# Linear attention with elu features: the first head's k loaded through ScalarE's DMA queue, at the same moment as its q through SyncE's

## Chip, cores, metric

One core of one Trainium2 chip. The metric is device time in microseconds (us), lower is better; a run counts as slow here when it is more than 1.5% above the fastest of its kernel. Positions such as "at 12 us" are counted from the start of the profiled span.

## The reference, cut

```
q, k, v: bf16 [1, 32 heads, 2048, 128]
phi_q = where(q > 0, q + 1, exp(q)) + 1e-6
phi_k = where(k > 0, k + 1, exp(k)) + 1e-6
kv  = einsum("bhsd,bhse->bhde", phi_k, v);   z = sum over s of phi_k
out = (phi_q @ kv) / (phi_q . z + 1e-6)
```

The kernel writes phi as min(exp(x), 1) + 1e-6 plus relu(x), so each head needs, for k and for q, an exponential (ACT), a min (DVE) and a relu.

## The kernel before: what matters here

Each engine has a fixed list of operations; waits are worked out from dependencies.

The operations (h is the head), with the line of the profile of before; in the profiles of the changed kernel each line number is higher by one:

```
ld*  SP    512 KB load into one of 7 buffers                         L324
T    PE    16 transposes of q                                        L368
eq   ACT   exp of the transposed q (PSUM)                            L372
ek   ACT   exp of k                                                  L336
em   DVE   min of k's exp (SBUF to SBUF)                             L339
emq  DVE   min of q's exp (SBUF to SBUF)                             L374
rkd  DVE   relu of k, first half (SBUF to SBUF)                      L342
rkp  POOL  relu of k, second half                                    L346
v1   POOL  copy of v beside a column of ones; for h >= 3 it also waits for r(h-3).0    L350
kv   PE    phi_k^T [v 1];   kvs ACT copies it to SBUF                L357, L362
n    PE    phi_q [kv z]; needs kvs and "ones"                        L389, L394, L396
r, f DVE   reciprocal; multiply (PSUM to SBUF)                       L403, L410
```

## Time and profile before

| | before |
|---|---|
| time, median of the runs of the first measurement | 170.62 us (169.57 to 170.72, 6 runs) |
| profiled run | 169.65 us, span 168.3 us |
| PE idle from 26 to 160 us | none |
| q, k, v of head 0 land | 4.2, 5.4, 7.7 us |

PE, DVE and ACT are all over 90% busy. From 26 us on PE never waits, so the end moves with whatever happens before that. The prediction below shows the lines.

### The profile page before, as it was taken

Reading aid. Unit: us, or ns where it says so; the run is one execution under the profiler, and the core shown is the slowest. Engines: PE = TensorE matmul, PEld = TensorE weight load, DVE = VectorE, ACT = ScalarE, POOL = GpSimd, SP = SyncE. Lnnn points to the kernel's source line nnn. Section 1 sums busy time; section 2 is a strip of 40 time slices with the busy share of each in tenths; the row PEclk is TensorE's granted clock in tenths of the full one; section 3 lists DMA queues with packets and bytes.
Section 4 is the critical chain, followed back from the end, with each engine's and each line's share of the span. In section 5 each row is a group of like instructions: output and inputs, shape, how many; then the busy total and the mean of one; then the engine's idle time right before and its main releaser. Section 6 shows DMA issues by size and latency. Waiting matters only on the chain.

```text
span 168.3 us, 6310 instructions
## 1 busy us (share of the span) xinstructions
PE 159.4 (95%) x2775; PEld 154.1 (92%) x2775; DVE 153.8 (91%) x267; ACT 153.7 (91%) x133; POOL 87.1 (52%) x71
## 2 busy tenths in 40 slices
PE   6999789999999999999999999999999999999960
PEld 2679779999999999999999999999999999999950
DVE  0177999999999999999999999999999999999894
ACT  3699989999999999999999999999999999998710
POOL 1436925556655555556555566556655565445000
PEclk9999999999999999999999999999999999999997
DMA  5999999999999999999999999999999999999986
GB/s 195 383 416 420 404 407 409 410 407 409 416 409 412 416 413 417 417 414 422 407 418 413 414 420 413 412 419 414 419 416 420 413 415 420 412 416 417 395 332 253
DMA packets 18748, 67.53 MB, mean 401 GB/s; under 512 B 2080, under 2 KB 2464, under 8 KB 18720
## 3 DMA queue, kind: packets, MB, share of 16 engines
q1 hardware_dynamic: 18720, 67.12, 98.9%
q8 instruction: 22, 0.36, 0.8%
q14 instruction: 6, 0.05, 0.1%
HBM read 50.33 MB, written 16.78 MB: 399 GB/s over the span
## 4 chain that ended last, share of the span: by engine, by line
PE 85%; DVE 8%; ACT 4%; issue 1%; POOL 0%; POOLq 0%
PE la L357 32%; PE la L394 18%; PE la L396 16%; PE la L368 16%; DVE la L410 4%; ACT la L336 2%; PE la L315 2%; DVE la L342 1%; DVE la L339 1%; ACT la L372 1%; PE la L389 1%; DVE la L403 1%; DVE la L381 1%; ACT la L378 1%; POOL la L301 0%
## 5 line engine op out<-in xcount | busy, mean ns | idle before, releaser
L410 DVE TENSOR_TENSOR la<-la 128x1536 bf16<-128x1536 f32 (+2 forms) x65 | 77.6, 1195 | 0.2
L396 PE MATMUL la<-la 128*128 128x129 bf16 x512 | 68.1, 220 | 0.0
L394 PE MATMUL la<-la 128*128 128x129 bf16 x512 | 68.0, 219 | 0.0
L372 ACT ACTIVATE la<-la 128x2048 bf16<-128x2048 bf16 (+2 forms) x35 | 60.3, 1732 | 5.7 <-PE la L368 3.8
L357 PE MATMUL la<-la 128*128 128x129 bf16 x1024 | 64.0, 219 | 0.7 <-DVE la L339 0.7
L350 POOL COPY la<-la 128x1024 int32<-128x1024 int32 (+1 forms) x33 | 41.9, 1273 | 38.1 <-DVE la L403 28.8
L336 ACT ACTIVATE la<-la 128x2048 bf16<-128x2048 bf16 (+1 forms) x33 | 61.4, 1863 | 0.0
L357 PEld LDWEIGHTS la<-la 128*128 128x128 bf16 x1024 | 60.0, 97 | 1.2 <-DVE la L339 0.8
L346 POOL TENSOR_SCALAR la<-la 128x1024 bf16<-128x1024 bf16 x32 | 44.5, 1393 | 29.1 <-DVE la L410 25.0
L396 PEld LDWEIGHTS la<-la 128*128 128x128 bf16 x512 | 49.5, 97 | 0.0
L394 PEld LDWEIGHTS la<-la 128*128 128x128 bf16 x512 | 47.1, 97 | 0.0
L368 PE MATMUL la<-la 128*128 128x128 bf16 x512 | 34.3, 221 | 0.4 <-DVE la L381 0.4
L389 PE MATMUL la<-la 128*128 128x3 bf16 (+1 forms) x192 | 32.3, 168 | 2.3 <-DVE la L410 1.6
L378 ACT ACTIVATE la<-la 128x1024 bf16<-128x1024 bf16 (+1 forms) x32 | 33.6, 1049 | 0.0
L368 PEld LDWEIGHTS la<-la 128*128 128x128 bf16 x512 | 29.9, 99 | 1.3 <-DVE la L381 0.5
L339 DVE TENSOR_SCALAR la<-la 128x2048 bf16<-128x2048 bf16 (+1 forms) x33 | 23.0, 696 | 3.6 <-ACT la L336 3.6
L389 PEld LDWEIGHTS la<-la 128*128 128x128 bf16 x192 | 18.7, 97 | 3.1 <-DVE la L410 2.0
L342 DVE TENSOR_SCALAR la<-la 128x1024 bf16<-128x1024 bf16 x32 | 17.1, 535 | 4.6 <-DMA la<-in_k_dram 4.6
L374 DVE TENSOR_SCALAR la<-la 128x2048 bf16<-128x2048 bf16 (+2 forms) x35 | 20.9, 599 | 0.3 <-ACT la L372 0.3
L381 DVE TENSOR_SCALAR la<-la 128x1024 bf16<-128x1024 bf16 x31 | 20.8, 671 | 0.0
L403 DVE RECIPROCAL la<-la 128x12 f32<-128x12 f32 (+2 forms) x65 | 12.8, 197 | 2.5 <-PE la L396 1.3
L362 ACT ACTIVATE la<-la 128x129 bf16<-128x129 f32 x32 | 9.1, 283 | 0.4 <-PE la L357 0.4
(14 smaller groups left out, 11.7 us busy)
## 6 DMA issues: line engine op xcount, KB each, us to landing
la<-in_q_dram SPq DMA_DIRECT2D x32, 512.0 KB, 15.5
la<-in_k_dram SPq DMA_DIRECT2D x32, 512.0 KB, 15.3
la<-in_v_dram SPq DMA_DIRECT2D x32, 512.0 KB, 15.3
out_dram<-la SPq DMA_DIRECT2D x31, 512.0 KB, 15.2
out_dram<-la SPq DMA_DIRECT2D x2, 192.0 KB, 2.5
out_dram<-la SPq DMA_DIRECT2D x1, 128.0 KB, 2.4
```

What stands on the lines that cost most here:

```text
L336: add("ACT", f"ek{h}.{i}", lambda e, a=a, b=b: e.activation(em_sb[:, h % NE, a:b], k_sb[:, h % NI, a:b], ACT.Exp), over("ldk", h, ld_parts ...
L339: add("DVE", f"em{h}.{i}", lambda e, a=a, b=b: e.tensor_scalar(em_sb[:, h % NE, a:b], em_sb[:, h % NE, a:b], 1.0, EPS, op0=ALU.min, op1=AL ...
L346: add("POOL", f"rkp{h}.{i}", lambda e, a=a, b=b: e.tensor_scalar(rk_sb[:, h % NR, a:b], k_sb[:, h % NI, a:b], BIG, 0.0, op0=ALU.min, op1=A ...
L350: add("POOL", f"v1{h}.{i}", lambda e, a=a, b=b: e.tensor_copy(v1_sb[:, h % NV, a:b, 0:D].bitcast(i32), v_sb[:, h % NI, a:b].bitcast(i32)), ...
L357: ins = e.matmul(kv_ps, lhsT=src[:, j], rhs=v1_sb[:, h % NV, j, 0:NC], start=(j + part == 0), stop=(j == NT - 1 and part == 1))
L368: ins = e.transpose(xT[:, j], q_sb[:, h % NI, j], ident[:])
L372: add("ACT", f"eq{h}.{i}", lambda e, a=a, b=b: e.activation(emq_sb[:, h % NQ, a:b], xT[:, a:b], ACT.Exp), over("T", h, t_parts, a, b) + fr ...
L378: add("ACT", f"rqa{h}", lambda e: e.activation(rq_sb[:, h % NQ, 0:n], xT[:, 0:n], ACT.Relu), over("T", h, t_parts, 0, n) + freed(NQ, h, (" ...
L389: e.matmul(_ap(o_ps[:, :], o + D, [[NC, m]]), lhsT=ones[:], rhs=epsr[:, 0:m], start=True, stop=False, skip_group_check=True)
L394: e.matmul(to, lhsT=emq_sb[:, h % NQ, t], rhs=kvs_sb[:, h % NK], start=False, stop=False, skip_group_check=True)
L396: ins = e.matmul(to, lhsT=rq_sb[:, h % NQ, t], rhs=kvs_sb[:, h % NK], start=False, stop=True, skip_group_check=True)
L410: return e.tensor_tensor(out=_ap(o_sb[:, :, :, :], first(o_sb[:, h % NO, t0, 0:1]) - first(o_sb[:, :, :, :]), [[m * D, nb], [D, m], [1, D] ...
```

## The change

The intent: q and k of head 0 are the first two things that are needed, and SyncE issues them one after the other, 0.42 us apart. ScalarE is free at the start, so it issues k at the moment at which SyncE issues q.

```diff
+BY_ACT = ('ldk0.0',)
 "ACT":
-        eq0.0 eq0.1 ek0.0 ek0.1 rqa0 ...
+        ldk0.0 eq0.0 eq0.1 ek0.0 ek0.1 rqa0 ...
 "SP":
-        ldq0.0 ldk0.0 ldv0.0 ldk1.0 ...
+        ldq0.0 ldv0.0 ldk1.0 ...
 def load(name, dst, src, h, i, t0, t1, last):
-            add("SP", f"ld{name}{h}.{i}", ...
+            add("ACT" if f"ld{name}{h}.{i}" in BY_ACT else "SP", f"ld{name}{h}.{i}", ...
```

More of the change, by code (lines that the diff above doesn't have):

```diff
@@ L115 @@
     "ACT": """
-        eq0.0 eq0.1 ek0.0 ek0.1 rqa0 ek1.0 kvs0 eq1.0 rqa1 ek2.0 kvs1 ek3.0 eq2.0 rqa2 kvs2 ek4.0 eq3.0 kvs3 rqa3
+        ldk0.0 eq0.0 eq0.1 ek0.0 ek0.1 rqa0 ek1.0 kvs0 eq1.0 rqa1 ek2.0 kvs1 ek3.0 eq2.0 rqa2 kvs2 ek4.0 eq3.0 kvs3 rqa3
         ek5.0 eq4.0 kvs4 rqa4 ek6.0 eq5.0 kvs5 rqa5 ek7.0 eq6.0 kvs6 rqa6 ek8.0 eq7.0 kvs7 rqa7 ek9.0 eq8.0 kvs8
@@ L132 @@
     "SP": """
-        ldq0.0 ldk0.0 ldv0.0 ldk1.0 ldq1.0 ldv1.0 ldk2.0 ldq2.0 ldk3.0 ldv2.0 ldv3.0 ldk4.0 ldq3.0 ldv4.0 ldq4.0
+        ldq0.0 ldv0.0 ldk1.0 ldq1.0 ldv1.0 ldk2.0 ldq2.0 ldk3.0 ldv2.0 ldv3.0 ldk4.0 ldq3.0 ldv4.0 ldq4.0
         ldk5.0 ldv5.0 ldk6.0 ldq5.0 ldv6.0 ldv7.0 ldk7.0 ldq6.0 ldk8.0 ldq7.0 ldk9.0 ldk10.0 ldq8.0 ldv8.0 ldv9.0
@@ L323, in load @@
         def load(name, dst, src, h, i, t0, t1, last):
-            add("SP", f"ld{name}{h}.{i}", lambda e: e.dma_start(dst[:, h % NI, t0:t1], rows(src, h)[:, t0:t1]),
+            add("ACT" if f"ld{name}{h}.{i}" in BY_ACT else "SP", f"ld{name}{h}.{i}", lambda e: e.dma_start(dst[:, h % NI, t0:t1], rows(src, h)[:, t0:t1]),
                 last, dma=f"{name}{h % NI}.{i}")
```

## The prediction

> **What bounds the kernel now.** I read the page first, then the table of stretches (busy time of each engine in each piece of the span), then the timeline of the first 24 us, then the landings of single DMAs.
>
> The page names PE as the chain that ended last, but three engines are almost equally full:
>
> ```profile
> PE 159.4 (95%) x2775; PEld 154.1 (92%) x2775; DVE 153.8 (91%) x267; ACT 153.7 (91%) x133; POOL 87.1 (52%) x71
> PE 85%; DVE 8%; ACT 4%; issue 1%; POOL 0%; POOLq 0%
> q1 hardware_dynamic: 18720, 67.12, 98.9%
> ```
>
> The table of stretches says where the slack is (columns: stretch, us, then busy us of PE, PEld, DVE, ACT, POOL, clock, DMA share, GB/s):
>
> ```profile
> 6.00:10.00 4.00, 4.00 (x33) 2.26 (x32) 0.84 (x3) 4.00 (x5) 1.94 (x3) 1.00 1.02 405
> 10.00:14.00 4.00, 3.59 (x66) 3.44 (x64) 2.75 (x10) 4.00 (x4) 2.41 (x2) 1.00 1.03 420
> ...
> 18.00:22.00 4.00, 3.34 (x58) 3.02 (x55) 4.00 (x5) 3.64 (x3) 2.87 (x3) 1.00 1.02 409
> 22.00:26.00 4.00, 3.47 (x60) 3.27 (x60) 3.96 (x8) 3.73 (x3) 1.16 (x2) 1.00 1.04 411
> ...
> 30.00:60.00 30.00, 30.00 (x551) 29.95 (x549) 29.80 (x52) 30.00 (x27) 17.68 (x13) 1.00 1.03 411
> ```
>
> From 26 us to 160 us PE has no idle time, so what moves the end is the moment at which PE becomes full, about 23.7 us. The change touches the first microseconds only. There ACT is the bound: from its first exponential at 5.80 us on it works without a pause until 21.6 us. What started it is in the timeline (start us, duration, engine, line, and in brackets the idle time before and who ended it):
>
> ```profile
> 0.74 0.37 SPq L324 DMA_DIRECT2D la<-in_q_dram  x1
> 1.16 0.42 SPq L324 DMA_DIRECT2D la<-in_k_dram  x1
> 1.53 3.38 PE L315 MATMUL la<-la 128*128 128x480 bf16 x8 [1.53 <-POOL la L301]
> 4.30 0.15 PEld L368 LDWEIGHTS la<-la 128*128 128x128 bf16 x1 [0.25 <-DMA la<-in_q_dram]
> 4.70 1.67 PE L368 MATMUL la<-la 128*128 128x128 bf16 x16
> 5.80 1.94 ACT L372 ACTIVATE la<-la 128x1024 bf16<-128x1024 bf16 x2 [3.78 <-PE la L368]
> 7.62 2.00 ACT L336 ACTIVATE la<-la 128x1024 bf16<-128x1024 bf16 x2
> ...
> 5.45 0.43 DVE L342 TENSOR_SCALAR la<-la 128x1024 bf16<-128x1024 bf16 x1 [4.55 <-DMA la<-in_k_dram]
> ```
>
> (The last line stands earlier in the timeline, by its start.) The reader is to see a chain: q of head 0 lands, PE transposes it (L368), ACT takes its exponential (L372), and only then, in ACT's fixed order, the exponential of k (L336) at 7.62. The landing times by tile are 3.5 us after issue for q (0.74 + 3.5 = 4.2 us), 4.3 for k (1.16 + 4.3 = 5.4) and 6.1 for v (1.63 + 6.1 = 7.7). So q has next to no slack: the weight load that needs it starts at 4.30, on the 0.40 us beat of the warm-up matmuls before it. k is used by ACT only at 7.62, and has 7.62 - 5.45 = 2.2 us of slack there; only two early relu halves (DVE L342 and GpSimd L346) start on its landing, and neither is on the chain.
>
> [...] The trace of before uses one data queue only (q1, 18720 packets)[...] it does show the engines full, 369 GB/s in 2.5 to 3 us and 401 GB/s in 3 to 4 us, so two transfers at once can't both be as fast as one alone. [...] the relu half of L342 takes 0.43 us at 5.45 and 1.26 us at 17.27 beside a GpSimd copy. [...] the 128x480 warm-up matmuls start 0.40 us apart at first, and 15 of them take 3.20 us (0.21 each) after 6.21.
>
> **The change, part by part.** It moves one instruction of 512 KB: k of head 0 leaves SyncE's list (second place) and becomes ACT's first instruction. Nothing is added; the count of DMAs and bytes stays. The instruction order of PE, DVE and GpSimd is the same.
>
> (1) Issue: k's issue moves from 1.16 to about 0.74 us, 0.42 us earlier, and every later SyncE issue comes about 0.45 us earlier. The DMA engines have work in hand from 1.8 us on (0.67 busy by 2.5 us, 1.01 in 3 to 4), so earlier issue brings at most a quicker ramp: in 1.8 to 3.0 us, at the 401 GB/s seen later, about 480 KB could move; seen are 0.4 us at 92, 0.5 at 221 and 0.5 at 369, or 332 KB. The lack of 150 KB is 0.37 us; I expect 0.1 to 0.2 of it back.
>
> (2) ACT: its table load (1.28 us, at 0.73 before) starts some 0.4 us later and ends near 2.5 us. Its first use is at 5.80: no cost.
>
> (3) q: now the two transfers start together and share. One DMA alone takes 512 KB / 0.41 MB per us = 1.28 us of the 16 engines. [...] q ends where the pair ends, at k's old landing of 5.42 less the ramp gain: 5.2 to 5.4 us, against 4.2 before. k gains nothing: it lands there too. v, third, has the same bytes ahead of it: 7.6 to 7.7 as before.
>
> (4) PE: the first transpose needs q. It starts at 4.91 in the chain of waits (4.70 in the timeline, under the last warm-up matmul). With q at 5.3 it starts at about 5.4, some 0.5 to 0.7 us late. Eight transposes at half clock take 0.87 us as before; ACT's first exponential starts at 6.3 to 6.5 in place of 5.80. So ACT's whole first stretch is **0.6 us late** (0.5 to 0.8).
>
> (5) What of it reaches the end. ACT works without idle to 21.6 us, so kvs, the first output matmuls and DVE's first reciprocal (14.32) shift by 0.6. But between 16.7 and 21.1 us DVE and GpSimd alternate: the GpSimd copy at 16.71 is released by the landing of the third head's v, which this change doesn't move, and DVE's L342 (1.26 where 0.43 is the free length), L339 (1.52, free 0.68) and L342 again (1.25) lose 0.83 + 0.84 + 0.82 = 2.5 us to it and its two successors. With DVE 0.6 us later, more of that copy lies beside DVE's PSUM work, which it doesn't disturb, so up to 0.6 us may be swallowed. ACT then has idle time of 0.44 (before L362 at 22.07) and 0.20 (before L372 at 24.35) that can take up 0.64 us if DVE isn't late. I take half as swallowed: of 0.6 us some 0.3 to 0.4 reaches PE's full stretch, and from there the end, unshortened. DMA doesn't gain or lose: it is full anyhow and buffered seven heads deep.
>
> Sum: 170.63 + 0.4 = **171.0 us**, or +0.2%.
>
> **Rivals.** (a) *SyncE's descriptors arrive first on all 16 engines*[...]. Then q lands at 4.2 to 4.3 as before, k at 5.4 or a little earlier, and nothing changes: 170.4 to 170.8. For it: ACT may take longer to issue than SyncE. Against: both are released from the starting barrier at the same moment (ACT's table load 0.73, SyncE's issue 0.74). (b) *All of the delay reaches the end*, or ACT's share goes first: +0.7 to +1.0, 171.3 to 171.6. For it: ACT and PE have no slack before 21 us in the table of stretches. Against: the GpSimd alternation above. (c) [...] a gap of half a microsecond in PE's warm-up, at 4.9 to 5.4 us[...]. Then the 15 warm-up matmuls ahead of the first kv take up to 0.40 in place of 0.21 us each, and the first kv (9.35 us) slips by up to 2 us: about 172.3. [...] (d) *Faster*: k early helps the chain. I see nothing for it: k is not awaited on the chain, and even a whole microsecond gained at the head would be 0.6%.
>
> **Range and chances.** Weights: partly swallowed 0.45 (around 171.0), no delay 0.2 (170.6), all of it 0.25 (171.4)[...]. The runs of before spread from 170.01 to 170.72, so a median of few runs is uncertain by 0.3. That gives 170.2 to 171.9 for 8 in 10. A change of 2% would be 3.4 us, which no rival reaches: faster 0.01, same 0.98, slower 0.01.
>
> **What would show the steps right or wrong.** Step 3 is right if q lands about 4.5 us after its issue (3.5 before), and k at 5.2 to 5.4 us; wrong if q still lands near 4.2. Step 4: ACT's first L372 starts at 6.3 to 6.5. Step 2: the table load ends by 3 us. Step 5: compare the start of kvs of the third head (L362 at 22.07) and of the last DVE multiply with ACT's lateness: if they are late by the full 0.6, nothing was swallowed; if by none, all was. The warm-up matmuls after the transposes must still take about 0.21 us each, else (c). The prediction is wrong if q is not delayed and the time still changes by over 0.5 us, or if the steady stretch from 26 us on shows PE idle.

## More of the kernel before

The starts of the lists (cuts marked with ...):

```
"PE":   w2 w1 T0.0 T0.1 w0 kv0.0 kv0.1 T1.0 n0.0 kv1.0 ...       # w: warm-up matmuls, WARM = (15, 4, 4)
"DVE":  v1ones0 rkd0.0 em0.0 eps0 em0.1 v1ones1 emq0.0 rqb0.0 emq0.1 eps1 rkd1.0 eps2 ones em1.0 r0.0 ...
        ... r24.1 rqb26.0 f24.1 r25.0 rkd28.0 emq26.0 f25.0 ...
"ACT":  eq0.0 eq0.1 ek0.0 ek0.1 rqa0 ek1.0 kvs0 eq1.0 ...
"POOL": ident0 ident rkp0.0 v10.0 v10.1 v11.0 rkp1.0 rkp2.0 v12.0 ...
"SP":   ldq0.0 ldk0.0 ldv0.0 ldk1.0 ldq1.0 ldv1.0 ...
```

One more view is needed afterwards: the timeline of DVE and GpSimd around 12 us in the kernel before (start us, duration us, engine, line, operation; in brackets the idle time before it and who ended it).

```profile
11.29 0.42 DVE L342 TENSOR_SCALAR la<-la 128x1024 bf16<-128x1024 bf16 x1
...
12.60 2.48 POOL L346 TENSOR_SCALAR la<-la 128x1024 bf16<-128x1024 bf16 x2
...
14.32 0.23 DVE L403 RECIPROCAL la<-la 128x12 f32<-128x12 f32 x1 [1.14 <-PE la L396]
```

DVE's relu of head 1 is over at 11.7 us, before GpSimd's relus begin at 12.60. The first reciprocal, which marks the end of the first group of head 0's output matmuls, starts at 14.32.

## The result

171.62 us median (171.50 to 171.86, 6 runs) against 170.62: ratio 1.0075, 95% interval 1.0048 to 1.0101. Ratios here are the mean time of one kernel's fast runs over that of the other's in the same rounds, so not quite the ratio of the quoted medians. The change makes the kernel slower by about 1 us, inside the range and within 2%, but by more than the 0.4 us predicted.

The page of the changed kernel, its busy shares and its queues (queue 10 is new, the k of head 0):

```profile
PE 159.0 (93%) x2775; PEld 153.4 (90%) x2775; DVE 155.1 (91%) x267; ACT 153.8 (90%) x133; POOL 86.5 (51%) x71
...
q10 hardware_dynamic: 144, 0.52, 0.8%
```

The start, in the timeline of the changed kernel:

```profile
0.73 0.40 ACTq L325 DMA_DIRECT2D la<-in_k_dram  x1
...
0.74 0.37 SPq L325 DMA_DIRECT2D la<-in_q_dram  x1
...
5.47 1.13 PE L369 MATMUL la<-la 128*128 128x128 bf16 x16 [0.56 <-DMA la<-in_q_dram]
5.63 0.43 DVE L343 TENSOR_SCALAR la<-la 128x1024 bf16<-128x1024 bf16 x1 [4.73 <-DMA la<-in_k_dram]
...
6.19 1.94 ACT L373 ACTIVATE la<-la 128x1024 bf16<-128x1024 bf16 x2 [3.74 <-PE la L369]
```

Both loads are issued together, and they share the DMA engines about evenly: from 3 to 4 us the profile counts 52 packets of queue 1 and 45 of queue 10, from 4 to 5 us 57 and 66. q lands 4.7 us after its issue in place of 3.5, at 5.43 us (the first of its 16 shares at 4.96; before, all 16 from 3.68 to 4.20); k lands at 5.60, and was at 5.42 before. Neither transfer gains, and the one that the chain waits for loses 1.2 us. PE now waits 0.56 us for q, and ACT starts at 6.19 in place of 5.80.

Then, around 12 us:

```profile
11.72 2.38 POOL L347 TENSOR_SCALAR la<-la 128x1024 bf16<-128x1024 bf16 x2
11.97 1.24 DVE L343 TENSOR_SCALAR la<-la 128x1024 bf16<-128x1024 bf16 x1
...
13.42 0.17 DVE L309 MEMSET la<- 128x128 bf16 x1
...
13.64 0.18 PE L390 MATMUL la<-la 128*128 128x3 bf16 x1 [1.07 <-DVE la L309]
...
15.31 0.23 DVE L404 RECIPROCAL la<-la 128x12 f32<-128x12 f32 x1 [0.66 <-PE la L397]
```

DVE's relu of head 1 is 0.68 us later than before (11.97), GpSimd's relus are 0.88 us earlier (11.72), because v of head 1 landed at 10.7 in place of 11.5 us. (The trace has 16 landings for each load. In the kernel before 14 shares of this v were there by 10.67 us too, two came at 11.45 and 11.54, and GpSimd's copy of it started at 11.59, after the last; in the changed kernel none lags.) Both shifts are needed for what follows: GpSimd's relu is now at work when DVE's comes, and DVE's takes 1.24 in place of 0.42 us, longer by about as much as the one that the prediction found beside a GpSimd copy at 17.27 us (1.26 us). The memset of the ones stands behind it in DVE's list, the output matmuls wait for it (L390 above), and the first reciprocal is late by 0.99 us: the 0.39 us of ACT have more than doubled. At the fifth multiply (29.59 against 28.86 us) 0.73 us is left, and that stays constant for 100 us.

At 137 us it grows again. The table of stretches (stretch, us, then busy us of PE, PEld, DVE, ACT, POOL, clock, DMA share, GB/s), before:

```profile
136.00:142.00 6.00, 6.00 (x113) 5.98 (x111) 5.92 (x13) 6.00 (x6) 2.93 (x3) 1.00 1.03 416
```

and after:

```profile
136.00:142.00 6.00, 5.37 (x99) 5.19 (x97) 6.00 (x10) 6.00 (x6) 2.93 (x3) 1.00 1.03 418
```

PE loses 0.63 us. The timeline of DVE and GpSimd there, before:

```profile
136.52 0.22 DVE L403 RECIPROCAL la<-la 128x12 f32<-128x12 f32 x1
...
136.94 0.68 DVE L374 TENSOR_SCALAR la<-la 128x2048 bf16<-128x2048 bf16 x1
...
137.03 1.48 POOL L350 COPY la<-la 128x1024 int32<-128x1024 int32 x1 [1.00 <-DVE la L342]
```

and after:

```profile
137.26 0.22 DVE L404 RECIPROCAL la<-la 128x12 f32<-128x12 f32 x1
...
137.55 1.10 POOL L351 COPY la<-la 128x1024 int32<-128x1024 int32 x1 [0.77 <-DVE la L404]
...
137.68 1.52 DVE L375 TENSOR_SCALAR la<-la 128x2048 bf16<-128x2048 bf16 x1
```

This is one race, won by the other side. GpSimd's copy for head 28 may start once the reciprocal r25.0 is done and its v has landed. That v lands at 136.91 us in both profiles. Before, the reciprocal was earlier (136.52), the copy waited for the landing and came at 137.03 (the view names DVE's relu L342, which ended last before it, but the copy doesn't depend on that relu), 0.09 us after DVE's min of q had started; DVE went first. In the changed kernel compute is 0.74 us later, the v is there already, the copy starts 0.29 us after the reciprocal and 0.13 us ahead of the min, and the min takes 1.52 in place of 0.68 us. From the 49th to the 57th multiply it is 19.70 us in place of 18.91.

The sum for the two profiled runs: 0.73 (start) + 0.79 (137 us) + 0.33 (from the start of the last multiply to the landing of the last store: 3.45 us in place of 3.12) = 1.85 us, the difference of the spans, 168.3 and 170.2. The medians differ by 1.0 only: the profiled run of before (169.65 us) was one of its fast ones, that of the changed kernel (171.50) an ordinary one. How the 1.0 us of the medians divides among these places is therefore not known.

### The profile page after: what moved, and what is told of

Same layout as the page of the kernel before. It is cut to its first block, busy times and chain, and to the rows that moved or that the text cites. A ratio compares the mean times of both kernels' runs of the same rounds, so it can differ in the third digit from the quotient of the medians.

```text
span 170.2 us, 6309 instructions
## 1 busy us (share of the span) xinstructions
PE 159.0 (93%) x2775; PEld 153.4 (90%) x2775; DVE 155.1 (91%) x267; ACT 153.8 (90%) x133; POOL 86.5 (51%) x71
## 4 chain that ended last, share of the span: by engine, by line
ACT 69%; PE 15%; DVE 10%; DMA 3%; issue 1%; DVEq 0%
ACT la L337 26%; ACT la L373 26%; ACT la L379 12%; PE la L358 6%; DVE la L411 4%; ACT la L363 4%; PE la L395 4%; PE la L397 3%; DMA la<-in_q_dram 3%; PE la L369 3%; DVE la L375 2%; DVE la L340 1%; DVE la L382 1%; DVE la L343 1%; DVE la L404 1%
## 5 line engine op out<-in xcount | busy, mean ns | idle before, releaser
L351 POOL COPY la<-la 128x1024 int32<-128x1024 int32 (+1 forms) x33 | 41.4, 1256 | 37.1 <-DVE la L404 30.0
L390 PE MATMUL la<-la 128*128 128x3 bf16 (+1 forms) x192 | 32.3, 168 | 3.6 <-DVE la L411 2.6
L369 PE MATMUL la<-la 128*128 128x128 bf16 x512 | 33.8, 219 | 0.6 <-DMA la<-in_q_dram 0.6
L390 PEld LDWEIGHTS la<-la 128*128 128x128 bf16 x192 | 18.7, 97 | 4.5 <-DVE la L411 3.1
L375 DVE TENSOR_SCALAR la<-la 128x2048 bf16<-128x2048 bf16 (+2 forms) x35 | 22.0, 632 | 0.3 <-ACT la L373 0.3
```

The lines of the kernel that those rows point to most:

```text
L351: add("POOL", f"v1{h}.{i}", lambda e, a=a, b=b: e.tensor_copy(v1_sb[:, h % NV, a:b, 0:D].bitcast(i32), v_sb[:, h % NI, a:b].bitcast(i32)), ...
L369: ins = e.transpose(xT[:, j], q_sb[:, h % NI, j], ident[:])
L375: add("DVE", f"emq{h}.{i}", lambda e, a=a, b=b: e.tensor_scalar(emq_sb[:, h % NQ, a:b], emq_sb[:, h % NQ, a:b], 1.0, EPS, op0=ALU.min, op1 ...
L390: e.matmul(_ap(o_ps[:, :], o + D, [[NC, m]]), lhsT=ones[:], rhs=epsr[:, 0:m], start=True, stop=False, skip_group_check=True)
```

## The experiments

Theory A: the late q costs 0.4 us at the start; two meetings multiply it, at 12 us and at 137 us (theory A2). A meeting is a DVE and a GpSimd operation between SBUF buffers at work at the same time, of which the second took longer than it does alone: DVE's relu 1.24 us in place of 0.42 at 12 us, its min of q 1.52 in place of 0.68 at 137 us. Rivals: the start differs by chance (B); ScalarE's queue costs by itself (E); the clock of PE becomes full late because of the gap in PE's work while it waits for q (theory A3). Other letters are explained in the expectations. The runs were made after the measurement above in three groups of four, each on another chip (b_again to a_rkd1, a_gate28 to a_hold, a_all to b_split). The kernel before took 170.09, 170.22 and 170.47 us there (medians of 11 runs each, 169.45 to 171.07 in all).

**b_again**: the kernel before, no edit.

> The kernel before, unchanged, timed against itself: ratio 1.000 within 0.3% by any theory. What it is for is a second profile. In the first profile (span 168.3 us, 169.65 us in all, a fast run of the spread 169.57 to 170.72) the first reciprocal of DVE starts at 14.32 us and two of the 16 shares of v of head 0 land 0.75 us after the others. Theory A (the loss of the change is made in the first 16 us: q late by 1.2 us, and then DVE and GpSimd colliding): the first reciprocal is again near 14.3 us, and the typical run is longer than the profiled one for another reason later in the span, e.g. a collision like the one at 137.7 us in the changed kernel. Rival B (the head differs from run to run and the profiles differ by chance): the first reciprocal moves by over 0.4 us.

Measured: 170.01 us (169.84 to 171.13), ratio 1.001 (0.998 to 1.004). First reciprocal at 14.32 us again, v of head 0 late again (8.07), no block at 137 us. The start of before is reproducible; rival B falls for it.

**a_again**: the changed kernel, no edit.

> The changed kernel, unchanged, for a second profile on the same chip. Theory A: time 1.006 to 1.009 of before; q of head 0 lands near 5.4 us, ACT starts at about 6.2 us, DVE's first relu of head 1 takes about 1.24 us beside GpSimd's, and the first reciprocal starts near 15.3 us, as in the first profile. Rival B: these places differ from the first profile by over 0.4 us. Also: does the long L375 (1.52 us in place of 0.68) at 137.7 us come again? If it does, it belongs to the schedule, if not it is chance.

Measured: 172.73 us (171.80 to 173.51), ratio 1.0164 (1.0135 to 1.0193): worse than expected, and scattered over 1.7 us. In its profile (171.80 us, its fastest run) q lands at 5.48, ACT starts at 6.60, not 6.2, and the first reciprocal at 15.68. The long min at 137 us is there again (19.69 us for the same stretch). So both meetings belong to the schedule; the later start is a third thing, seen in PE's lines: 16 transposes took 1.89 us here and 1.13 in the first profile. The trace's record of the granted clock has it begin to be full at 7.33 us, against 5.64.

**a_consts**: the memsets out from behind the blocked relu.

```diff
-v1ones0 rkd0.0 em0.0 eps0 em0.1 v1ones1 emq0.0 rqb0.0 emq0.1 eps1 rkd1.0 eps2 ones em1.0
+v1ones0 eps0 eps1 eps2 ones v1ones1 rkd0.0 em0.0 em0.1 emq0.0 rqb0.0 emq0.1 rkd1.0 em1.0
```

> The changed kernel, with DVE's memsets of the eps row and of the ones moved to the front of its list, where it is idle until 5.6 us. In the changed kernel the ones (13.42 us) stand behind the relu half of head 1 that is blocked for 0.8 us, and the first output matmul waits for them until 13.6 us, although kvs was done at 12.8. Theory A (the delay of 0.4 us grows to 1.0 us because of that block): the first reciprocal comes 0.4 to 0.5 us earlier (14.8 to 14.9) and the time falls by 0.3 to 0.5 us, to 1.004 of before. Rival C (the blocked DVE is the bound there, not the ones): the output matmuls start earlier, but the time stays within 0.15 us of the changed kernel's.

Measured: 171.17 us (170.35 to 173.22), ratio 1.0066 (1.003 to 1.010), 1% below a_again of the same rounds. But the profile fell on its one run of the slow state (173.22): q at 5.76, full clock only at 10.6 us, the 15 warm-up matmuls 4.74 in place of 3.20 us, the first reciprocal at 16.46. The expectation for the reciprocal could not be read; the gain in time is larger than expected and lies in a wide scatter. Inconclusive.

**a_rkd1**: DVE's relu of head 1 moved into its idle time, away from GpSimd's.

```diff
-v1ones0 rkd0.0 em0.0 ... emq0.1 eps1 rkd1.0 eps2 ones em1.0
+v1ones0 rkd0.0 rkd1.0 em0.0 ... emq0.1 eps1 eps2 ones em1.0
```

> The changed kernel, with DVE's relu half of head 1 moved to just after that of head 0, into DVE's idle time before 9.1 us (its k lands at 8.1 us), so that it does not meet GpSimd's relu at 11.7 us. Theory A: the first reciprocal at 14.6 to 14.9 us in place of 15.3, DVE free of the 0.8 us block, and the time 0.4 to 0.6 us below the changed kernel's: 1.003 to 1.005 of before, which leaves the 0.4 us of the late q. Rival C (what happens before 16 us is swallowed later): no change, 1.007. Rival D (the block only moves to the next DVE instruction, the min of head 1 beside the same GpSimd relu): first reciprocal earlier, time within 0.15 us of the changed kernel's.

Measured: 171.18 us (170.02 to 172.93), ratio 1.006 (1.002 to 1.010), 1% below a_again, with one run (172.93) slow and left out of the ratio. The timeline of DVE:

```profile
8.21 0.43 DVE L343 TENSOR_SCALAR la<-la 128x1024 bf16<-128x1024 bf16 x1 [2.18 <-DMA la<-in_k_dram]
...
12.35 0.17 DVE L309 MEMSET la<- 128x128 bf16 x1
...
14.79 0.23 DVE L404 RECIPROCAL la<-la 128x12 f32<-128x12 f32 x1 [1.23 <-PE la L397]
```

ACT starts at 6.27, 0.47 us later than before, and the reciprocal is now late by just that, 0.47 us, in place of 0.99. At the fifth multiply 0.20 us is left (29.06), in place of 0.73. So up to there the block at 12 us is worth 0.5 us and the late q itself 0.2 us. The meeting at 137 us still comes (19.68 us). Over the whole run this profile shows no gain over the first one of the changed kernel, though: the last multiply starts 0.43 us earlier, but from there to the last landing it takes 3.84 us in place of 3.45, and the span is 170.2 us in both.

**a_gate28**: one wait of GpSimd, head 28 only.

```diff
 def gate(name, h):
+    if name == "v1" and h == 28:
+        return ["emq26.0"]
     return [f"r{h - 3}.0"] if name == "v1" else [f"f{h - 3}.0"]
```

> The changed kernel; GpSimd's copy of v for head 28 waits for DVE's min of q of head 26 in place of the reciprocal before it, nothing else. Theory A2: all profiles of the changed kernel so far lose 0.79 us at 137 us (20th to 28th pair of multiplies: 19.7 us in place of 18.9)[...]; in the kernel before the same copy is held by the landing of its v (136.91 us) until that min has begun. So here the min takes 0.7 us again, the stretch takes 18.9 us and the time falls by 0.6 to 0.8 us against the changed kernel. Rival: the loss turns up at the next meeting of the two engines; then the time stays.

Measured: 170.85 us (five runs 170.71 to 170.97, one 172.31), ratio 1.0056 (1.002 to 1.009). The timeline (here L377 is the min of q, L353 the copy):

```profile
137.97 0.68 DVE L377 TENSOR_SCALAR la<-la 128x2048 bf16<-128x2048 bf16 x1
...
138.72 1.04 POOL L353 COPY la<-la 128x1024 int32<-128x1024 int32 x1 [1.65 <-DVE la L377]
```

The min takes 0.68 us, the stretch 18.91 us, and nothing is lost further on (13.47 us for the eight multiplies after it, as in before), though its start is late (reciprocal at 15.61, 15.31 in the first profile). The loss at 137 us is that one race, as theory A2 has it. The changed kernel itself was not in these rounds; the nearest to it there, a_warm, has a median 0.73 us higher, which fits, but the intervals of the two ratios overlap.

**b_gate28**: the same edit in the kernel before.

> The kernel before with the same single wait changed. Its runs lie between 169.4 and 171.1 us. Theory A2: in the profiled runs (168.3 and 168.6 us) v of head 28 landed late enough (136.91 and 137.19, reciprocal at 136.5 and 136.7) for DVE to go first, so these gain nothing; runs in which compute is over 0.3 us later [...] are 0.8 us longer. So the upper runs vanish: median 169.8 to 169.9, highest below 170.3; ratio 0.997 to 1.000. If the upper runs stay, they have another cause (the start, for one).

Measured: 170.03 us (169.70 to 170.23), ratio 0.9992 (0.997 to 1.0015). None of 6 runs lies above 170.23; 5 of the 11 runs of before in the same rounds lie above 170.3. That would fit the theory that before loses the race in part of its runs, but the mean doesn't move measurably, and no profile of one of before's longer runs was had. The one profile here doesn't support it: compute was 0.64 us late at the 49th multiply, but v of head 28 landed 0.64 us later too (137.55), after the reciprocal (137.16). With the 0.12 us from landing to copy seen in before, the copy would have come at about 137.67 (an estimate) without the edit, behind the min (137.58). Not a faster kernel; at most a steadier one.

**a_warm**: two more warm-up matmuls ahead of the transposes.

```diff
-WARM = (15, 4, 4)
+WARM = (15, 5, 5)
```

> The changed kernel with ten warm-up matmuls ahead of the first transposes in place of eight, so that PE is busy until 5.7 us and the gap at 4.9 to 5.4 us, in which PE waits for the late q, is filled. Theory A3: on the second chip the changed kernel's runs spread from 171.8 to 173.5 us, and two profiles have PE's full clock begin at 7.3 and 10.6 us in place of 5.6 to 6.0[...]. With the gap filled the spread closes to 0.6 us or less, at 171.5 to 172.0. Rival: the spread has nothing to do with the gap and stays above 1 us.

Measured: 171.58 us (171.47 to 172.38), ratio 1.0094 (1.007 to 1.012). Five of six runs within 0.2 us, the sixth 0.8 above; a_again scattered over 1.7 us, on another chip. The spread did not close to the 0.6 us expected, and that the gap has a part in the scatter isn't shown: the first six runs of the changed kernel, whose profile has the gap, lie within 0.36 us.

**a_hold**: k by ScalarE, 0.76 us after q.

```diff
-load("k", k_sb, kf, h, i, a, b, freed(...))
+load("k", k_sb, kf, h, i, a, b, (["ident"] if h == 0 else []) + freed(...))
```

> The changed kernel, with ScalarE's issue of k held until GpSimd has made the identity (1.47 us), 0.7 us after SyncE's issue of q: the other queue is used, but not at the same moment. Theory A (q shares the engines with what is in flight beside it): q lands at 4.3 to 4.8 us, ACT starts at 5.8 to 6.0, PE has no gap worth counting, and the time is within 0.3% of the kernel before. Rival E (the use of ScalarE's queue costs in itself[...]): the time stays 0.6% or more above before, with q on time.

Measured: 171.85 us (171.23 to 173.48), ratio 1.012 (1.008 to 1.016). A miss; its profile, of the slowest run, shows where. q landed at 4.08 us and ACT started at 5.80, as in before: used at another moment, ScalarE's queue does q no harm. But v of head 0, issued by SyncE at 1.17, was ahead of k, issued at 1.50: queue 10 has no packet before 4.5 us, when v was nearly done (it landed at 5.31). 15 of the 16 shares of k landed by 7.46, the last one at 8.33 us. The chain broke at the next link:

```profile
8.35 2.00 ACT L337 ACTIVATE la<-la 128x1024 bf16<-128x1024 bf16 x2 [0.61 <-DMA la<-in_k_dram]
```

In this profile the full clock began at 7.46 us although PE had no gap, so a late clock comes without a gap too. Rival E is not decided by this run.

**a_all**: a_rkd1, a_gate28 and a_warm together, on the changed kernel.

> The changed kernel with three repairs together: DVE's relu half of head 1 early (no meeting with GpSimd at 12 us), the wait of the copy for head 28 (no meeting at 137 us), and two more warm-up matmuls (no gap in PE while q is late). Theory: these are the three places where the late q turns into time, so only the swallowed lateness stays: first reciprocal 14.7 to 14.9 us, fifth multiply at 29.0 to 29.2 us, 18.9 us for the stretch of heads 24 to 28, and a time within 0.2% of the kernel before (169.9 to 170.5 us). Rival: a fourth cause; then 0.4% or more above before stays.

Measured: 170.75 us (169.88 to 171.14), ratio 1.0013 (0.998 to 1.005): the time agrees with the theory, the path only in part. The profile is of the slowest run: with ten warm-up matmuls and a clock that is full only at 6.79 us ACT starts at 6.60, the block moves to DVE's min of q (1.27 us at 10.84, beside the copy of v), and the reciprocal comes at 15.40, not 14.8. The stretch at 137 us is 18.92. So rival D of a_rkd1, that a block only moves on, is true for some starts. A control is missing: of the three repairs only the wait of head 28 was tried on the kernel before, so the other two may be worth something there as well.

**b_kfirst**: before, with k first and q second on SyncE's queue.

```diff
-        ldq0.0 ldk0.0 ldv0.0 ldk1.0 ...
+        ldk0.0 ldq0.0 ldv0.0 ldk1.0 ...
```

> The kernel before, all on SyncE's queue, with the loads of q and k of head 0 exchanged: k first, then q. No use of ScalarE's queue. Theory A (a late q makes the loss, the queue doesn't matter): q lands at 5.3 to 5.5 us, ACT starts at 6.1 to 6.6 us, and the time is above before, by 0.3 to 1.0%. Whether the block at 12 us comes depends on v: in the profiles of before, v of head 1 lands at 11.5 to 12.1 us, in those of the changed kernel at 10.7. If here it lands at 11.5 again, GpSimd's relu comes after DVE's, the first reciprocal is at 14.7 to 14.9 us and the loss is 0.2 to 0.4 us plus 0.8 us at 137 us. Rival E (ScalarE's queue itself): time as before, within 0.2%.

Measured: 170.89 us (169.96 to 171.20), ratio 1.0023 (0.999 to 1.005). q lands at 5.27, ACT starts at 6.39; v of head 1 lands at 10.8 us, not 11.5, DVE's relu takes 1.24 us, the reciprocal comes at 15.47, the fifth multiply at 29.75, and the min at 137 us takes 1.52. So each step of the path, the late q, the block at 12 us and the race at 137 us, comes without a second queue. The time is less clear: the interval includes no loss at all, and a_swap below, with ScalarE's queue and a late q in the same rounds, is 0.8% longer (1.006 to 1.014 against 0.999 to 1.005). Part of that stands at the end: from the start of the last multiply to the last landing it takes 2.74 us here; in the changed kernel 3.45, in a_swap 3.42. That the late q alone makes the whole loss is not shown.

**a_swap**: q by ScalarE, k by SyncE, at the same moment (the two names are also exchanged in the lists of ACT and SP, cut here).

```diff
-BY_ACT = ('ldk0.0',)
+BY_ACT = ('ldq0.0',)
```

> The changed kernel with the two first loads exchanged between the queues: q of head 0 through ScalarE's, k through SyncE's, at the same moment. Theory A [...]: q lands at 5.3 to 5.7 us as in the changed kernel, and the time is within 0.4% of the changed kernel's, 1.006 to 1.012 of before. Rival F (one queue goes first, ScalarE's for instance): q lands near 4.2 us, k at 5.4, and the time is that of before.

Measured: 171.76 us (171.62 to 172.97), ratio 1.010 (1.006 to 1.014). q lands 5.2 us after its issue, at 5.91, k at 5.73. Whichever queue has q, both transfers are late, and ScalarE's lands last, by 0.17 us in the first profile of the changed kernel and by 0.18 us here. Rival F falls.

**b_split**: an attempt at a faster start: before with the wait of b_gate28, q of head 0 in two halves, five warm-up matmuls ahead of the transposes (cut to two of its edits).

```diff
-WARM = (15, 4, 4)
+WARM = (15, 2, 3)
-        ldq0.0 ldk0.0 ldv0.0 ...
+        ldq0.0 ldq0.1 ldk0.0 ldv0.0 ...
```

> The kernel before with the changed wait for head 28, and q of head 0 loaded in two halves through SyncE's queue, with five warm-up matmuls before the first transposes in place of eight, so that these can start when the first half lands. Theory A (the landing of q and the warm-up before it set the start of ACT's saturated stretch): the first half lands near 3.6 us, ACT starts at 4.5 to 4.8 us in place of 5.8, its second exponential at 5.6; the first reciprocal comes 0.5 to 1.0 us earlier and the time falls by 0.2 to 0.7 us, to 0.996 to 0.999 of before, since near the end the DMA engines, which finish st30 at 167.0 us of 168.3, leave less than a microsecond to gain. Rival: later landings (v of heads 1 and 2) hold the start of PE's full stretch where it is: 1.000.

Measured: 171.34 us (171.19 to 171.50), ratio 1.0058 (1.003 to 1.0085). The first half landed at 3.39 us and ACT started at 4.59, as expected; but k of head 0 landed only at 7.65 us (5.42 before), ACT waited 1.12 us for it, and the first reciprocal came at 14.36, where it was. Even so the fifth multiply was 0.46 us ahead of before (28.40 us). The time was lost after that, in three more meetings: DVE's mins of k at 44.2, 54.1 and 154.3 us took 1.08, 1.22 and 1.37 us in place of 0.68, each beside a copy of v that had waited for its landing and started 0.2 to 0.5 us ahead of the min. The first of them (here L345 is the min of k, L356 the copy):

```profile
43.72 1.04 POOL L356 COPY la<-la 128x1024 int32<-128x1024 int32 x1 [2.65 <-DMA la<-in_v_dram]
44.22 1.08 DVE L345 TENSOR_SCALAR la<-la 128x2048 bf16<-128x2048 bf16 x1
```

The last multiply is 1.35 us late. Why six of k's 16 shares landed up to 1.7 us after the other ten is not explained.

## Why the prediction was right or wrong

The time lay in the range, and the sign and the class were right. That the time lay in the range is partly luck: the range was put together from four courses, and none of them has the two meetings that made most of the loss in the profiled pair. By its steps:

1. Issue: earlier issue bought even less than the 0.1 to 0.2 us expected, nothing: k landed 0.18 us later than before. (The sum behind it compares the bytes moved from 1.6 to 3.0 us with those possible from 1.8 to 3.0.) v of head 0 did come earlier (6.83, where 7.6 to 7.7 was predicted), but not through the issue: with k first on one queue it was at 6.96. In before two of v's 16 shares lag 0.75 us behind the rest, and so it goes on in the loads after it, v of head 1 among them; why they don't when q is second is open.
2. Table load: right. It started at 1.16 us, took 1.28, and nobody waited.
3. Sharing: right in kind and size, though with one data queue in the trace of before it was the estimate that the two would share (q at 5.2 to 5.4 predicted, 5.43 measured, and 5.2 to 5.9 in the seven other profiles in which both are issued together).
4. PE and ACT: the transposes started 0.56 us late, as predicted (0.5 to 0.7); for ACT 0.6 us was predicted, and it was 0.39 in the first profile, 0.35 to 1.08 in the others with both loads at once. In the first profile the eight transposes took 0.70 us, where 0.87 was assumed, with the full clock beginning at 5.64 us. (In before the eight lie ahead of its full clock, which begins at 5.99 us; with it, from 26 us on, sixteen take 0.91 or 0.92 us in the chain.)
5. **The step that failed** is in (5): "kvs, the first output matmuls and DVE's first reciprocal (14.32) shift by 0.6", that is, by ACT's lateness and no more. ACT was 0.39 us late and the first reciprocal 0.99, through a meeting at 12 us that the kernel before does not have. In a_rkd1, where that meeting is taken away, both are 0.47 late, as the step has it. That GpSimd's copy doesn't disturb DVE's PSUM work, on which the term "I take half as swallowed" rests, the trace of before shows: 26 multiplies (128x1536) that start while a copy is at work take 1.74 to 1.75 us, three with no GpSimd operation beside them 1.74 to 1.76, and 27 relus of q (L381) wholly beside GpSimd's relu 0.66 to 0.68, two alone 0.68 and 0.69. The term was about right in size: from the first to the fifth multiply 0.26 us of the lateness was made up (0.99 to 0.73; in a_rkd1 0.47 to 0.21), where 0.3 was predicted. But the same 0.26 or 0.27 was made up in all ten profiles with a late q or k, however late it was, so it isn't shown that this happened in the way that the prediction gives. The prediction looked at meetings that exist already (16.7 to 21 us), not for new ones that the shift makes. By its own test nothing was swallowed: kvs of the third head came at 23.07, 1.00 us late, and the last multiply 1.52 us late.
6. "From there the end, unshortened" was wrong too: the same lateness lost one more race at 137 us, for 0.79 us (a_gate28). The prediction named PE idle after 26 us as a sign that it is wrong, and the profile shows it, 0.63 us.

Of the rivals, (a) and (d) fell; (b) was nearest in size, though not by its mechanism; (c), a late clock, which had a weight of 0.1, comes in part of the runs: the full clock came at 7.3 and 7.5 us in the profiles of a_again and b_kfirst (10.6 in the slow run of a_consts). That the gap causes it is not shown: a_swap has the longest gap (1.05 us) and a full clock at 5.45 us, a_hold has no gap and 7.46.

Open: the last 0.33 us, at the end. In all nine profiles of kernels that use ScalarE's queue the time from the start of the last multiply to the last landing is 3.39 us or more; with one queue it is 2.74 to 3.21, except for b_split (3.63). In the changed kernel one of the 16 shares of the last store lands at 170.15 us and the other 15 by 169.34; what delays that one is not shown. This is the part of rival E that stands, and by the times of b_kfirst and a_swap it may be larger than 0.33 us; against a large cost of the queue in itself speaks a_all, which uses it and lies 0.1% above before.

## What to carry to other kernels

Two loads issued at once, where one queue already kept the DMA engines busy (401 GB/s from 3 to 4 us in before), both landed when the second would have (5.43 and 5.60 us here, 5.42 for the second before): issue first and alone what the chain needs first. In a schedule tuned to the last tenth of a microsecond a shift isn't added or swallowed, it is raced: look at the operations of the two engines of which the second takes longer when they meet (by 0.82 and 0.84 us here) and ask which of them the shift puts first, where the distance in the profile is small (here 0.09 us before, 0.13 us after). A transfer that lands earlier can lose such a race as well as one that lands later, and so can a kernel that starts earlier (b_split was 0.46 us ahead and its profiled span ended up 1.9 us longer than that of before).
